# The first steps of a fused attention, mixing and FFT kernel in another order: x ahead of the weights, taps by ScalarE's queue, signs by ScalarE

## The chip, the core and the metric

The kernel runs on one core of one Trainium2 chip. The metric is the device time of one execution in microseconds; for the kernel before there are three runs, and their median counts. A core has engines that each work through their own list of instructions in order: TensorE (PE: matmuls, and PEld: the loads of their weights), VectorE (DVE), ScalarE (ACT), GpSimd (POOL) and SyncE (SP), which here only issues DMA transfers. ScalarE issues some transfers too; in rows of the profile such an issue is marked ACTq, one of SyncE SPq. An instruction that waits for another engine or a transfer holds up everything behind it on its own engine.

## The reference, cut to what matters

```python
B, S, D = 4, 4224, 192
# 1: softmax over 7 taps of 8 heads, a causal convolution of each head's 24 channels
w = softmax(weight)                           # (8, 7)
x = einsum('hk,bskhg->bshg', w, windows(x))   # (4, 4224, 192)
# 2: token mixing of rank 32, then an MLP 192 -> 768 -> 192
h = x^T @ U @ V                               # U (4224, 32), V (32, 4224)
u = x + h^T
x = u + relu(u @ moe_w_ch1) @ moe_w_ch2
# 3: real part of a 2D FFT over sequence and channels, layer norm, a second MLP
u = x + real(fft(fft(x, axis=1), axis=2))
out = u + relu(norm(u) @ moe2_w_ch1) @ moe2_w_ch2
```

The weights of the MLPs, U and V come in as float64, in two 32-bit words each, and the kernel makes float32 of them by integer operations ("decoding").

## The kernel before

Work is cut by batch b (4) and by block j of 384 tokens (11 per batch). For each pair the MLP of stage 2 (s = 0) and, later, of stage 3 (s = 1) runs as one block: layer 1 is six units of matmuls with 384 columns (L665, L655), whose results ScalarE evicts with a relu in half precision (L650) and VectorE as the rest (L651); layer 2 is three units of matmuls with 192 columns (L697 to L701), which VectorE adds to the tokens (L704). Each float32 operand is split into a high and a low half-precision part.

Before the first block can run, much has to be made, and this start is what the change touches:

- The convolution. The taps' softmax runs on single-row tiles (L983 to L989); the row is written to DRAM (L991) and read back as a shifted matrix `tap` by two loads (L995). x comes in three chunks per batch (`load_x`, L159, 14, 14 and 10 columns; three buffers, so chunk 0 of batch 1 takes the buffer of chunk 0 of batch 0). A chunk is convolved in four units (L398, 16 rows of matmuls each), ScalarE evicts each unit in place (L404), and the chunk is stored to DRAM as `x1d` (L368). A gunit (L414) multiplies a chunk by U; VectorE sums the three (L419, L421); `gfin` (L427, L431) replicates the sum.
- A block (`pre1`) loads its tokens from `x1d` (`pre_load`, L504), adds h (matmul L522, add L525), takes the sizes (ScalarE, L543), the scales (L547, L550), the normalised copy and its high half (ScalarE, L555, L578), the low half (GpSimd, L561), and transposes both by DMA (L585) into `ch`, which layer 1 reads.
- Decoding (`decode`, L162): five VectorE instructions per piece of up to 384 columns: the sign taken off (L172), a clamp (L175), a shift (L176) and two merges (L178, L179). A weight piece is followed by its maximum (L223). `weights_units(0)` makes from this the scale (L230 to L243; the maximum over partitions takes a matmul, L121) and the splits: split1h, split1e (ScalarE, L257) and split1a, split1b (VectorE, L264, L286 to L296) for w1, split2 for w2.

The order of all this is written by hand. `play(0)` goes through the words of `START[0]`; a word like c4 takes four steps from the queue c (convolution of batch 0), d is batch 1's convolution, w the weights' steps, a and b the first and second block's steps, e the split of V; X, U, V, P, Y, L are loads, A0 and s0 the stores of the first 4 and the other 10 columns of chunk 0, u0, u1, v0 decodings, B0 and B1 (`busy`) idle matmuls that fill TensorE's waits, as the `WARM` matmuls at the very start do. `START[t]` for t > 0 is played between the units of the blocks. The program order of each engine follows from it; what two engines owe each other is awaited where the later one stands in its list. ScalarE issues A0 in the kernel before; SyncE issues all else here.

Of the kernel before, what the change touches and what calls it, by code (L numbers as in the profile page):

```python
# [6 lines left out]
F32 = mybir.dt.float32  # L7
# [37 lines left out]
WARM = 52  # L45
AGAIN = (18, 44)
# [51 lines left out]
def build(tc, io):  # L98
# [30 lines left out]
    with tc.manual_schedule():  # L129
# [32 lines left out]
        def decode(raw, out):  # L162

            p, n = raw.shape[0], raw.shape[1]
            if n > DN:
                decode(raw[:, :DN], out[:, :DN])
                decode(raw[:, DN:], out[:, DN:])
                return
            lo, hi = raw[:, :, 0], raw[:, :, 1]
            t = wrk.tile([P, DN], I32, name="dec", bufs=1)[:p, :n]  # L170
            g, h = nc.vector.tensor_scalar, nc.vector.scalar_tensor_tensor
            g(out=t, in0=hi, scalar1=0x7FFFFFFF, scalar2=None, op0=ALU.bitwise_and)  # L172

            f = t.bitcast(F32)
            g(out=f, in0=f, scalar1=W_MIN, scalar2=W_MAX, op0=ALU.max, op1=ALU.min)  # L175
# [13 lines left out]
        def weights_units(i):  # L189
# [31 lines left out]
            def dec(a, z, n):  # L221
                decode(st["raw"][:, a:z], st["w"][:, a:z])
                nc.vector.tensor_reduce(out=st["mx"][:, n:n + 1], in_=st["w"][:, a:z],  # L223
                                        axis=AX.X, op=ALU.max, apply_absolute_value=True)
# [83 lines left out]
            if i == 0:  # L308
# [3 lines left out]
                                       lambda: scaled(0, FF + FH, 0), split1h, split1e, split1a, split1b] + \  # L312
# [188 lines left out]
        def pre_load(b, j):  # L501
            t = wrk.tile([P, TB, D], F32, name="u", tag="u", bufs=5)
            src = x1d[b]
            nc.sync.dma_start(  # L504
# [455 lines left out]
        part = w0_st["st"]["part"]  # L960
        part(0)
        load_uv("u", 0, UH)
# [28 lines left out]
        nc.sync.dma_start(rowd[:, nz:KC * H], rowt[:, nz:])  # L991

        load_x(0, 0)
        for i in range(2):
            nc.sync.dma_start(tap[KC * i:KC * i + KC].rearrange("p o h -> p (o h)"), bass.AP(  # L995
# [5 lines left out]
        def dec_u(n):  # L1001
            sl = slice(n * UH, (n + 1) * UH)
            decode(uv["u"][:, sl], uf[:, sl])

        def dec_v(a, z):
# [8 lines left out]
                    s0=lambda: stores[0](0, FIRST), A0=lambda: stores[0](0, 0, FIRST, nc.scalar))  # L1014
        for n in range(4):
            jobs.update({f"X{n}": lambda n=n: load_x(0, n), f"Y{n}": lambda n=n: load_x(1, n),
                         f"P{n}": lambda n=n: part(n), f"L{n}": lambda n=n: ahead_load(n),
                         f"s{n + 1}": lambda n=n: stores[0](n + 1),                          f"u{n}": lambda n=n: dec_u(n)})

        def play(t):  # L1020
# [117 lines left out]
```

## Time and profile before

| what | us |
|---|---|
| median of 3 runs | 1028.82 |
| lowest, highest | 1028.32, 1030.73 |
| profiled execution: span from first to last instruction | 1017.3 |
| TensorE busy | 979.1 |
| VectorE busy | 748.4 |
| ScalarE busy | 604.4 |
| GpSimd busy | 380.9 |

The whole device time of the profiled execution isn't given beside its span; the median is 11.5 us above that span. A row of a timeline gives the start, the duration, the engine, the line, the operation, the written tile and the read ones, the shapes, and in brackets how long the engine had been idle before and what ended it. The chain of waits is the work that ended last, followed back from the end: at each step what released it.

### The profile page before, as it was taken

What the parts mean: (1) busy time and instruction counts of PE and PEld (TensorE: products, weight loads), DVE (VectorE), ACT (ScalarE), POOL (GpSimd) and SP (SyncE); (2) the same over time, 40 slices, a digit from 0 to 9 for tenths busy, and PEclk for the clock granted to TensorE, in tenths of its full rate; (3) what the DMA queues carried; (4) which work ended last, traced back from release to release, by engine and by line L of the source; (5) the groups of instructions that cost most, each with busy time, mean ns of one, the idle gap of its engine ahead of it and who ended that gap; (6) DMA issues with size and microseconds to landing.
All of it is one profiled execution on the core that took longest, in us unless ns stands there. A gap on an engine that the chain in (4) does not pass through costs nothing.

```text
span 1017.3 us, 25682 instructions
## 1 busy us (share of the span) xinstructions
PE 979.1 (96%) x9929; PEld 764.8 (75%) x9929; DVE 748.4 (74%) x2094; ACT 604.4 (59%) x1512; POOL 380.9 (37%) x397
## 2 busy tenths in 40 slices
PE   8789898999899999999999999998999999999998
PEld 5466676777677777877778887776888877877776
DVE  7766577689876656687776777897789787766663
ACT  2556554765676666656576666655656665555552
POOL 0111111253552344265534445564157651562110
PEclk9999999999999999999999999999999999999999
DMA  7596857685536666443425455433344332542332
GB/s 288 155 230 183 252 148 189 178 213 158 151 99 154 203 201 179 114 138 101 102 73 146 134 155 139 108 87 82 87 131 110 107 87 65 137 110 68 82 72 63
DMA packets 190804, 139.28 MB, mean 137 GB/s; under 512 B 128186, under 2 KB 164257, under 8 KB 189913
## 3 DMA queue, kind: packets, MB, share of 16 engines
q1 hardware_dynamic: 183095, 124.59, 45.6%
q0 software_dynamic: 7104, 12.70, 4.8%
q8 instruction: 77, 1.26, 0.5%
q14 instruction: 46, 0.38, 0.1%
q10 hardware_dynamic: 482, 0.35, 0.1%
HBM read 61.69 MB, written 46.11 MB: 106 GB/s over the span
## 4 chain that ended last, share of the span: by engine, by line
PE 62%; DVE 12%; DMA 11%; POOL 5%; issue 5%; ACT 4%; SPq 0%; DVEq 0%; ACTq 0%; POOLq 0%
PE l L665 24%; PE l L697 9%; PE l L701 8%; PE l L699 8%; PE l L655 5%; DMA ch<-sp 4%; DVE hl L651 3%; DMA xm<-x2d,mrow 2%; POOL xm L756 2%; PE cv L398 2%; PE sd L863 2%; PE s L879 2%; DMA x1d<-xw 1%; DVE x L790 1%; POOL xp L804 1%
## 5 line engine op out<-in xcount | busy, mean ns | idle before, releaser
L665 PE MATMUL l<-ch,w1h 128*128 128x384 f16 x1584 | 407.2, 327 | 15.4 <-DMA ch<-sp 10.1
L697 PE MATMUL l<-w2h,hh 128*128 128x192 f16 x1584 | 391.9, 247 | 5.8 <-DVE hl L651 4.5
L699 PE MATMUL l<-w2l,hh 128*128 128x192 f16 x1584 | 391.4, 247 | 1.2 <-DVE w2l L264 1.2
L701 PE MATMUL l<-w2h,hl 128*128 128x192 f16 x1584 | 391.4, 247 | 0.5 <-DVE hl L651 0.4
L651 DVE SCALAR_TENSOR_TENSOR hl<-l,hh 128x384 f16<-128x384 f32 x528 | 267.6, 549 | 127.2 <-ACT hh L650 126.1
L650 ACT ACTIVATE hh<-l 128x384 f16<-128x384 f32 x528 | 235.3, 494 | 155.7 <-PE l L655 155.3
L665 PEld LDWEIGHTS <-w1h 128*128 128x128 f16 x1584 | 155.1, 98 | 106.8 <-DMA ch<-sp 12.3
L697 PEld LDWEIGHTS <-hh 128*128 128x128 f16 x1584 | 155.6, 98 | 23.1 <-issue 12.3
L665 PE MATMUL l<-ch,w1l 128*128 128x384 f16 x528 | 172.7, 327 | 0.0
L699 PEld LDWEIGHTS <-hh 128*128 128x128 f16 x1584 | 155.7, 98 | 17.1 <-issue 6.5
L701 PEld LDWEIGHTS <-hl 128*128 128x128 f16 x1584 | 155.7, 98 | 3.1 <-DVE hl L651 1.4
L561 POOL TENSOR_TENSOR sp<-un,sp 128x576 f16<-128x576 f32 x44 | 57.3, 1302 | 250.4 <-ACT sp L578 228.3
L655 PE MATMUL l<-ch,w1l 128*128 128x384 f16 (+1 forms) x528 | 133.9, 327 | 0.0
L756 POOL DMA_INDIRECT xm<-x2d,mrow x84 | 84.9, 1011 | 21.3 <-issue 17.8
L631 POOL TENSOR_TENSOR sp<-un,sp 128x576 f16<-128x576 f32 x34 | 44.9, 1320 | 120.2 <-ACT sp L578 118.9
L625 ACT ACTIVATE un<-u,mr,rs 128x192 f32<-128x192 f32 x132 | 62.4, 537 | 25.3 <-DVE mr L619 24.7
L555 ACT ACTIVATE un<-u,rc 128x192 f32<-128x192 f32 x132 | 50.2, 445 | 43.0 <-DVE rc L550 43.0
L704 DVE SCALAR_TENSOR_TENSOR u<-l,cmax,u 128x192 f32<-128x192 f32 x132 | 54.5, 413 | 25.5 <-PE l L701 20.9
L665 PEld LDWEIGHTS <-w1l 128*128 128x128 f16 x528 | 51.8, 98 | 28.0 <-issue 4.0
L543 ACT ACTIVATE junk<-u 128x192 f16<-128x192 f32 x132 | 47.7, 361 | 40.6 <-DVE u L534 24.2
L849 POOL DMA_INDIRECT u<-x2d,mrow x64 | 62.4, 975 | 15.3 <-issue 11.7
L704 DVE SCALAR_TENSOR_TENSOR u<-l,ws,u 128x192 f32<-128x192 f32 x132 | 53.9, 410 | 18.2 <-PE l L701 18.0
(136 smaller groups left out, 1189.5 us busy)
## 6 DMA issues: line engine op xcount, KB each, us to landing
x2d<-u SPq DMA_DIRECT2D x68, 288.0 KB
u<-x1d SPq DMA_DIRECT2D x44, 288.0 KB
out_d<-u SPq DMA_DIRECT2D x43, 288.0 KB
x1d<-xw SPq DMA_DIRECT2D x36, 210.0 KB
u<-x2d SPq DMA_DIRECT2D x32, 192.0 KB
x<-x2d SPq DMA_DIRECT2D x60, 99.0 KB
xw<-x_d SPq DMA_DIRECT2D x4, 1344.0 KB
xw<-x_d SPq DMA_DIRECT2D x8, 672.0 KB
```

The costliest lines, as they stand in the source:

```text
L561: low_engine(0, b, j).tensor_tensor(out=sp[:, :, D:2 * D], in0=k["un"], in1=sp[:, :, :D], op=ALU.subtract)
L625: nc.scalar.activation(un[:, t], u[:, t], AF.Identity, scale=k["r"][:, t:t + 1], bias=k["m"][:, t:t + 1])
L650: nc.scalar.activation(hh[:, m], acc[m], AF.Relu)
L651: nc.vector.scalar_tensor_tensor(out=hl[:, m], in0=acc[m], scalar=0.0, in1=hh[:, m], op0=ALU.max, op1=ALU.subtract)
L655: nc.tensor.matmul(acc[m].rearrange("p (r n) -> p r n", r=TB), lhsT=w["l1"][rows, n, m * P:(m + 1) * P], rhs=kd[x][rows], start=False, sto ...
L665: nc.tensor.matmul(o, lhsT=w[v][:, e, ms], rhs=kd[x], start=(n == 0), stop=False)
L697: nc.tensor.matmul(o, lhsT=hh[:, m, rs], rhs=w["h2"][:, m], start=(m == 0), stop=False)
L699: nc.tensor.matmul(o, lhsT=hh[:, m, rs], rhs=w["l2"][:, m], start=False, stop=False)
L701: nc.tensor.matmul(o, lhsT=hl[:, m, rs], rhs=w["h2"][:, m], start=False, stop=(m == NM - 1))
L704: nc.vector.scalar_tensor_tensor(out=u[:, r], in0=o, scalar=sc, in1=u[:, r], op0=ALU.mult, op1=ALU.add)
L756: nc.gpsimd.indirect_dma_start(out=xs[c][1][:, g], out_offset=None, in_=x2d[b][:], in_offset=bass.IndirectOffsetOnAxis(ap=mrow[:99, k:k + ...
L849: nc.gpsimd.indirect_dma_start(out=u2[:, s0 + 2 * e], out_offset=None, in_=src[:], in_offset=bass.IndirectOffsetOnAxis(ap=mrow[:, k2 + e - ...
```

## The change

- x chunk 0 and the first half of U are loaded ahead of the first weights.
- The row of taps and the two loads of taps are issued by ScalarE's queue instead of SyncE's; so is the load of block 0's tokens (L0).
- In the decoding of the first three weight pieces and of U the sign is taken off by ScalarE (Abs) instead of VectorE; the decoding's scratch tile has two buffers instead of one.
- `START` has another order: the loads of x chunks 1 and 2 and of V ahead of the third weight piece's, w2's load (P2) right behind the stores, chunk 1's stores and chunk 0 of batch 1 (Y0) early, the third piece and its scale behind the second gunit, split1a ahead of split1e, four units of batch 1's convolution (d2 twice) ahead of the first block, w2's scale and split one step earlier.
- `WARM` is 42 for 52 matmuls, the second filler 30 for 44.

```diff
-WARM = 52
-AGAIN = (18, 44)
+WARM = 42
+AGAIN = (18, 30)
...
-        def decode(raw, out):
+        def decode(raw, out, first=False):
...
-            t = wrk.tile([P, DN], I32, name="dec", bufs=1)[:p, :n]
+            t = wrk.tile([P, DN], I32, name="dec", bufs=2)[:p, :n]
             g, h = nc.vector.tensor_scalar, nc.vector.scalar_tensor_tensor
-            g(out=t, in0=hi, scalar1=0x7FFFFFFF, scalar2=None, op0=ALU.bitwise_and)
-
             f = t.bitcast(F32)
+            if first:
+                nc.scalar.activation(f, hi.bitcast(F32), AF.Abs)
+            else:
+                g(out=t, in0=hi, scalar1=0x7FFFFFFF, scalar2=None, op0=ALU.bitwise_and)
...
-                decode(st["raw"][:, a:z], st["w"][:, a:z])
+                decode(st["raw"][:, a:z], st["w"][:, a:z], i == 0 and z <= FF + FH)
...
-                                       lambda: scaled(0, FF + FH, 0), split1h, split1e, split1a, split1b] + \
+                                       lambda: scaled(0, FF + FH, 0), split1h, split1a, split1e, split1b] + \
...
-        def pre_load(b, j):
+        def pre_load(b, j, eng=nc.sync):
...
         part = w0_st["st"]["part"]
+        load_x(0, 0)
+        load_uv("u", 0, UH)
         part(0)
-        load_uv("u", 0, UH)
...
-        nc.sync.dma_start(rowd[:, nz:KC * H], rowt[:, nz:])
-
-        load_x(0, 0)
+        nc.scalar.dma_start(rowd[:, nz:KC * H], rowt[:, nz:])
         for i in range(2):
-            nc.sync.dma_start(tap[KC * i:KC * i + KC].rearrange("p o h -> p (o h)"), bass.AP(
+            nc.scalar.dma_start(tap[KC * i:KC * i + KC].rearrange("p o h -> p (o h)"), bass.AP(
...
-            decode(uv["u"][:, sl], uf[:, sl])
+            decode(uv["u"][:, sl], uf[:, sl], True)
...
+                    L0=lambda: pre_load(0, 0, nc.scalar))
...
         START = [
-            "S U1 P1 X1 X2 V w2 u0 c4 B0 A0 L0 s0 L1 P2 u1 w c5 w3 v0 c4 w c3 w2 a4 w a4 b2 B1 w b4 w L2 b2 w",
-            "w s1", "", "w2 L3 V12", "w s2", "Y0", "z", "", "z", "d", "d Y1", "d", "d z", "d", "d z", "d Y2", "d e", "d", "d e", "d e",
-            "d e", "d e", "d e", "d", "d e", "d e", "d e", "d"]
+            "X1 U1 S X2 V P1 u0 w2 c4 B0 A0 s0 P2 L0 u1 c5 L1 s1 Y0 v0 c4 w c2 w3 c w a3 w a5 w2 B1 b4 w b4 w d2 w L2 d2",
+            "w2", "", "w2 L3 V12", "s2", "Y1", "z", "", "z", "d", "d", "d z Y2", "d", "d z", "d", "d e", "d", "d e", "d", "d e",
+            "d e", "d e", "e", "d", "e", "d e", "e"]
```

## Rows read from the trace of the kernel before

**Rows 1.** The page's first part: busy time, share of the span, instructions.

```profile
PE 979.1 (96%) x9929; PEld 764.8 (75%) x9929; DVE 748.4 (74%) x2094; ACT 604.4 (59%) x1512; POOL 380.9 (37%) x397
```

**Rows 2.** Stretches: length, busy time of each engine, TensorE's granted clock, DMA share, GB/s.

```profile
42.20:60.00 17.80, 13.51 (x87) 8.28 (x87) 15.03 (x40) 11.46 (x31) 2.56 (x2) 0.95 0.67 187
60.00:70.00 10.00, 8.70 (x81) 7.18 (x79) 6.68 (x20) 3.28 (x9) 0.02 (x1) 0.91 1.10 266
```

**Rows 3.** Timeline of TensorE: a filler, and starts after a wait.

```profile
16.09 3.10 PE L975 MATMUL l<-hl 128*128 128x384 f16 x18
...
42.20 0.32 PE L665 MATMUL l<-ch,w1h 128*128 128x384 f16 x1 [2.67 <-DMA ch<-sp]
...
58.30 0.29 PE L699 MATMUL l<-w2l,hh 128*128 128x192 f16 x1 [1.21 <-DVE w2l L264]
...
65.78 0.34 PE L665 MATMUL l<-ch,w1h 128*128 128x384 f16 x1 [1.30 <-DVE xmax L712]
```

**Rows 4.** The chain of waits in order of time: start, length, what.

```profile
4.48 2.02 DMA rowd<-hh
...
7.19 6.36 DMA tap<-rowd
13.59 0.92 PE cv L398 x15
```

**Rows 5.** Timeline of ScalarE.

```profile
14.49 2.85 ACT L404 ACTIVATE xw<-cv 128x336 f32<-128x336 f32 x8 [10.97 <-PE cv L398]
17.37 1.77 ACTq L368 DMA_DIRECT2D x1d<-xw  x2
...
31.20 1.29 ACT L257 ACTIVATE w1h<-u,sc 64x384 f16<-64x384 f32 x2
...
35.48 1.15 ACT L555 ACTIVATE un<-u,rc 128x192 f32<-128x192 f32 x3 [1.54 <-DVE rc L550]
36.65 0.68 ACT L578 ACTIVATE sp<-un 128x576 f16<-128x576 f32 x1
```

**Rows 6.** Timeline of SyncE's queue: the load of block 0.

```profile
24.49 0.33 SPq L504 DMA_DIRECT2D u<-x1d  x1
```

**Rows 7.** Waits of SyncE's queue up to 60 us: total, times, longest.

```profile
SPq L504 <- DMA x1d<-xw: 19.7, 3, 10.5
...
SPq L159 <- DMA xw<-x_d: 1.9, 1, 1.9
```

**Rows 8.** DMA from 17.4 to 20.7 us: the only queue with data packets.

```profile
q1 hardware_dynamic: 207, 1.31, 95.4%
```

**Rows 9.** DMA from 20.7 to 24.4 us: ScalarE's queue (q10) and SyncE's (q1).

```profile
q10 hardware_dynamic: 476, 0.34, 27.7%
q1 hardware_dynamic: 122, 0.34, 22.8%
```

**Rows 10.** Timeline of VectorE: the decoding and its waits.

```profile
5.15 0.36 DVE L172 TENSOR_SCALAR dec<-u 128x384 int32<-128x384 int32 x1 [0.70 <-DMA u<-wa_d]
...
10.90 0.35 DVE L172 TENSOR_SCALAR dec<-u 128x384 int32<-128x384 int32 x1
...
15.52 0.36 DVE L172 TENSOR_SCALAR dec<-u 128x384 int32<-128x384 int32 x1 [0.51 <-DMA u<-u_d]
...
24.35 0.36 DVE L419 COPY gacc<-gp 128x192 f32<-128x192 f32 x1 [1.75 <-PE gp L414]
...
25.37 0.29 DVE L122 TENSOR_REDUCE ma<-am 128x1 f32<-128x128 f32 x1 [0.60 <-PE am L121]
...
28.95 0.36 DVE L421 TENSOR_TENSOR gacc<-gp,gacc 128x192 f32<-128x192 f32 x1 [0.67 <-PE gp L414]
29.93 0.36 DVE L421 TENSOR_TENSOR gacc<-gp,gacc 128x192 f32<-128x192 f32 x1 [0.62 <-PE gp L414]
...
39.67 0.36 DVE L172 TENSOR_SCALAR dec<-u 128x384 int32<-128x384 int32 x1 [3.44 <-DMA u<-wc_d]
...
48.48 0.55 DVE L223 TENSOR_REDUCE mx<-u 128x1 f32<-128x384 f32 x1
...
56.83 1.42 DVE L264 SCALAR_TENSOR_TENSOR w2l<-u,sc,w2h 128x1152 f16<-128x1152 f32 x1 [2.28 <-ACT w2h L257]
```

**Rows 11.** An Abs on ScalarE (its timeline); a convolution unit of batch 1 (chain).

```profile
32.51 0.36 ACT L543 ACTIVATE junk<-u 128x192 f16<-128x192 f32 x1
...
78.96 0.79 PE cv L398 x16
```

More of the change, by code (lines that the diff above doesn't have):

```diff
@@ L159, in load_x @@
             nc.sync.dma_start(xw_t[b, c][:, ks], io["x"][b, c][:, ks])
-        def decode(raw, out):
+        def decode(raw, out, first=False):
             p, n = raw.shape[0], raw.shape[1]
             if n > DN:
-                decode(raw[:, :DN], out[:, :DN])
-                decode(raw[:, DN:], out[:, DN:])
+                decode(raw[:, :DN], out[:, :DN], first)
+                decode(raw[:, DN:], out[:, DN:], first)
                 return
             lo, hi = raw[:, :, 0], raw[:, :, 1]
-            t = wrk.tile([P, DN], I32, name="dec", bufs=1)[:p, :n]
+            t = wrk.tile([P, DN], I32, name="dec", bufs=2)[:p, :n]
             g, h = nc.vector.tensor_scalar, nc.vector.scalar_tensor_tensor
-            g(out=t, in0=hi, scalar1=0x7FFFFFFF, scalar2=None, op0=ALU.bitwise_and)
             f = t.bitcast(F32)
+            if first:
+                nc.scalar.activation(f, hi.bitcast(F32), AF.Abs)
+            else:
+                g(out=t, in0=hi, scalar1=0x7FFFFFFF, scalar2=None, op0=ALU.bitwise_and)
             g(out=f, in0=f, scalar1=W_MIN, scalar2=W_MAX, op0=ALU.max, op1=ALU.min)
@@ L499, in build @@
         xmax = {}
-        def pre_load(b, j):
+        def pre_load(b, j, eng=nc.sync):
             t = wrk.tile([P, TB, D], F32, name="u", tag="u", bufs=5)
             src = x1d[b]
-            nc.sync.dma_start(
+            eng.dma_start(
                 t, src[j * TB * P:(j + 1) * TB * P].rearrange("(p r) d -> p r d", r=TB))
@@ L1013, in build @@
                     U1=lambda: load_uv("u", UH, 2 * UH),
-                    s0=lambda: stores[0](0, FIRST), A0=lambda: stores[0](0, 0, FIRST, nc.scalar))
+                    s0=lambda: stores[0](0, FIRST), A0=lambda: stores[0](0, 0, FIRST, nc.scalar),
+                    L0=lambda: pre_load(0, 0, nc.scalar))
         for n in range(4):
             jobs.update({f"X{n}": lambda n=n: load_x(0, n), f"Y{n}": lambda n=n: load_x(1, n),
-                         f"P{n}": lambda n=n: part(n), f"L{n}": lambda n=n: ahead_load(n),
+                         f"P{n}": lambda n=n: part(n), f"L{n + 1}": lambda n=n: ahead_load(n + 1),
                          f"s{n + 1}": lambda n=n: stores[0](n + 1),                          f"u{n}": lambda n=n: dec_u(n)})
```

## Prediction

> **What bounds the kernel now.** I read the page first: TensorE is busy for 96% of the span [rows 1], so after its start the kernel can only gain what TensorE no longer has to do. The stretches come next: between 42.20 and 60.00 us TensorE is busy for 13.51 of 17.80 us and its granted clock is 0.95, so some of that stretch ran at 1.2 GHz and the rest at 2.4 GHz [rows 2]. Then TensorE's timeline: the first layer-1 matmul starts at 42.20 us, the second layer gets going only at 58.30 us, when VectorE's low half of w2 is there, and one more wait of 1.30 us ends at 65.78 us [rows 3]. Everything that is moved lies ahead of 58.30 us, so the question is when that point comes, and how much work for TensorE is left after it.
>
> Two chains lead there. The chain of waits shows the first: the row of taps takes 2.02 us to DRAM, and the two tap loads that follow it hold the first convolution until 13.59 us, 6.36 us after the second was issued [rows 4]. ScalarE empties the four units (14.49 to 17.34 us) and issues the first two stores at 17.37 us [rows 5]; SyncE, which must see them landed before it may load block 0, gets past them at 24.49 us [rows 6], a wait of 10.5 us for that load alone [rows 7]. The second chain is VectorE. From 15.52 us to 49.03 us (the last maximum, 48.48 plus 0.55) it does one long list: half of U, the third weight piece, V, the splits, the adds of two blocks, three pieces of w2. In it are waits of 1.75, 0.60, 0.67, 0.62 and 3.44 us [rows 10], 7.08 us in all, so 26.43 us are work.
>
> **Part by part.**
>
> *x first, taps on ScalarE's queue.* x chunk 0 is no longer behind two loads, but the convolution needs the taps as well, and those set its start. Their row can't leave before the softmax is done, which nothing here makes earlier: 4.48 us as before [rows 4]. The warm-up has 10 matmuls fewer; 18 of the same kind took 3.10 us at the full granted clock [rows 3], so that is 1.7 us, and TensorE is free at about 11.1 us instead of 12.8. That is the lower end of the convolution's start. The upper end is not given by 13.59 us alone: the taps now share the DMA engines with the loads that SyncE has already queued, instead of standing behind x chunk 0 only. How such a transfer fares is seen once: of the two stores that ScalarE's queue issued at 17.37 us, no packet at all moved until 20.7 us, while SyncE's queue moved 207 [rows 8]; from then both moved [rows 9]. So about 3.3 us pass before the first packet. Twice 3.3 us (the row of taps, then the taps) on 4.48 us, with their landing, gives 12 to 14 us. I take 12.5 us, 1.1 us earlier than now; bounds 11.1 and, with more queued ahead, 17.5 us.
>
> *Stores and the load of block 0 on ScalarE's queue.* ScalarE issues the stores 3.78 us after the convolution's start (13.59 to 17.37) [rows 4, 5], that is at 16.3 us. The load of block 0 now stands behind them on **ScalarE** and waits there for their landing, and so does all that ScalarE has queued next: the signs of the second half of U and the eight evictions of x chunk 1. That is the new wait. Before, it was SyncE that stood still, with the remaining stores of chunk 0 and w2 behind it. Its price: the same two stores took 7.12 us from issue to the next step (17.37 to 24.49) [rows 5, 6]; the nearest lower bound is the tiny row of taps, 2.02 us [rows 4]. I take 7.1 us, the row of the very same transfers, since SyncE's queue is full at that time in the new order as well. ScalarE goes on at 23.4 us; bounds 18.3 and 24.5 us, or 28 with the late taps.
>
> *Signs by ScalarE.* Seven VectorE instructions of 0.28 to 0.36 us go (three weight pieces, two halves of U with two pieces each). What they cost on ScalarE is bounded by the 0.36 us of an Abs of half the width [rows 11] and twice that; I take 0.5 us. Up to 23.4 us VectorE has the first half of U and two weight pieces. Before, the two weight pieces took 5.75 us (5.15 to 10.90) and half of U 4.11 us (10.90 to 15.01) [rows 10]; without the signs 5.0 and 3.4 us. Begun when ScalarE has issued the taps, at about 8.5 us, they end at 17 us. VectorE then **stands still for about 6.9 us**, because its next job, the other half of U, waits for its sign.
>
> *VectorE's list from there.* It is the same list as from 15.52 to 49.03 us: 26.43 us of work less three signs (1.1 us), 25.35 us. Its waits are others. w2 now leaves SyncE's queue right behind the stores and lands long before it is wanted, so the 3.44 us are gone. The waits for the gunits' matmuls (1.75, 0.67, 0.62) are covered by V and the third weight piece. New are 0.5 us for the first sign of U, 0.5 us for that of the third piece, 0.6 us for the maximum's matmul (as before), about 0.8 us for the chain from the last add to block 0's add, which the split no longer covers, and the wait for the split of the two ends, which ScalarE now does after block 0's normalised copy: 1.15 + 0.68 + 1.29 us [rows 5], of which I count 2.8. That is 5.2 us. The list ends at 23.4 + 25.35 + 5.2 = 54.0 us, **5.0 us later** than 49.03.
>
> *From the list's end to TensorE's steady work.* Before, 9.27 us (49.03 to 58.30). In the new order w2's scale and split come one step earlier, which can save up to the 1.42 us of that split [rows 10]; against it the eight evictions of the moved convolution units, 2.85 us on ScalarE [rows 5], stand ahead of the first relus. Bounds -1.4 and +2.9 us; I take +1.2.
>
> *Work moved ahead.* Four units of batch 1's convolution now run before the first block. Each took 0.79 us in TensorE's chain [rows 11], so 4 x 0.79 = **3.2 us less** is left after that point; TensorE waits there anyway, so they cost nothing if chunk 0 of batch 1 has landed by then; its load stands behind chunk 1's stores, and if it comes late the first layer waits for it, and the 3.2 us are the bound of that too. The shorter second filler (30 for 44) is idle work in the same wait: nothing.
>
> *The wait at 65.78 us.* It was VectorE's backlog behind the late split of w2; with that split a step earlier I let it go: -1.3 us; bounds -1.3 and 0.
>
> **Sum**: +5.0 +1.2 -3.2 -1.3 = +1.7 us on a span of 1017.3 us. What lies around the span is 1028.82 - 1017.3 = 11.5 us, if the profiled execution is like the median of the three runs, and nothing there is touched. So 1028.82 + 1.7 = 1030.5 us. About 0.3%, 3.1 us, is what a measurement of this kernel can tell from no change; this is inside it.
>
> **The rivals.**
>
> *Faster: the stores land soon.* The Trainium skill, "DMA: Bandwidth & Descriptors", section "Queues, rings and completion order", says that a DMA engine goes round-robin between the queue rows that have work, a packet at a time. [Rows 8] speak against that for the first 3.3 us, [rows 9] for it afterwards. As a mechanism of this kernel: if ScalarE's transfers get their share at once, the taps are there when the warm-up ends (11.1 us), the stores leave at 14.9 us and land in about 3.7 us, the length of the stretch in which they moved [rows 9], at 18.6 us. ScalarE goes on 4.8 us earlier than in my sum: 1025.7 us. If TensorE then has no stretch at 1.2 GHz between 42 and 70 us, another 0.05 x 17.8 + 0.09 x 10 = 1.8 us could come back [rows 2]; with half of that, **1024.8 us**. It decides for itself where ScalarE goes on before about 19 us.
>
> *Slower: the taps come late.* SyncE waited 1.9 us with a load of x for an earlier load of x that has its own tile [rows 7]: a transfer waits for one some places ahead of it, whatever they hold. In the new order five or six large loads are issued ahead of the taps. If a tap load waits for x chunk 1 in this way, or the engines take up SyncE's queued loads first, the convolution starts at 17.5 us instead of 12.5 and all that follows moves by 5 us: **1035.5 us**. For it: the taps sat behind everything that was ahead of them before as well. Against: rows 9, and that 3.3 us is what was seen. It decides where the convolution starts after about 14 us.
>
> *The change doesn't do what it says*: x is first, but the taps gate the convolution. That is already part of my sum; it gives 1.1 us.
>
> **How the numbers follow.** My own case, 1030.5 us with a range of 1027.5 to 1033, gets 0.42; faster 0.28 at 1024.8; slower 0.30 at 1035.5. The part of my case above 1031.9 and that of the slower case below it are about equal. So faster by over 0.3% 0.28, within 0.3% 0.41, slower by over 0.3% 0.31. The range reaches into both rivals and leaves 1 in 10 out on each side: 1023.5 to 1037.
>
> **What would show it.** On ScalarE's timeline: the load of block 0 issued some 7 us after the two stores, and nothing between. On VectorE: a wait of 5 to 8 us that a sign of the second half of U ends, and no wait for w2. The first convolution at 11 to 14 us. The last maximum of w2 near 54 us. TensorE's second layer from about 64 to 66 us, and four convolution units of batch 1 ahead of the first layer-1 matmul. My sum is wrong if ScalarE goes on before 19 or after 26 us, or if VectorE's list, from that sign on, isn't about 30 us long.

## The result, and the profile after

| | median, us | lowest to highest | profiled execution: its time, span |
|---|---|---|---|
| before | 1029.78 | 1028.32 to 1035.2 | not given, 1017.3 |
| after | 1041.2 | 1040.38 to 1042.84 | 1040.38, 1038.6 |

The ratio is 1.0105, interval 1.0067 to 1.0144: the change costs 0.0105 x 1029.78 = 10.8 us. I had forecast +1.7 us and a range that ended at 1037.

The two spans differ by 21 us, not by 11. What lies around the span of after is 1040.38 - 1038.6 = 1.8 us (1.7 to 2.7 in all other runs). If it is as much before, the 11.5 us of my sum were no time around the span: the profiled execution of before was 1028.82 - 1017.3 - 1.8 = 9.7 us quicker than the median beside it. Chips differ: the kernel before had a median of 1028 us on one and of 1015 to 1017 us on three others. Below, ratios compare runs of the same chip, and a second pair of traces, before (span 1026.2) and after (1039.3) on one chip, stands for the first where a difference of few us matters.

Timeline of TensorE after, three starts that a wait precedes (start, length, what, in brackets the idle time and what ended it):

```profile
15.96 5.64 PE L400 MATMUL cv<-xw,tap 64*64 64x168 f32 x64 [5.65 <-DMA tap<-rowd]
...
57.51 0.48 PE L667 MATMUL l<-ch,w1h 128*128 128x384 f16 x1 [4.51 <-ACT xw L406]
...
62.44 0.77 PE L121 MATMUL am<-sel,mx 128*128 128x128 f32 x2 [1.57 <-DVE mx L232]
```

Before, the first convolution began at 13.59 us and the first layer-1 matmul at 42.20 [rows 3, 4]. The convolution took 2.57 us there and takes 5.64 here. The stretches (length, busy time of each engine, granted clock, DMA share, GB/s) say why: the clock is 0.50, that is 1.2 GHz, after 5.65 us in which TensorE had nothing to do; and it is 0.50 again as the blocks begin (before, 0.95 and 0.91 between 42 and 70 us [rows 2]).

```profile
16.20:20.30 4.10, 4.03 (x54) 3.08 (x57) 2.39 (x6) 1.59 (x4) 0.00 (x0) 0.50 0.98 392
...
56.70:66.90 10.20, 7.82 (x27) 3.63 (x27) 7.38 (x20) 4.51 (x12) 1.28 (x1) 0.50 0.67 186
```

ScalarE's timeline after shows the new wait. The stores leave at 22.45 us (17.37 before [rows 5]), the load of block 0 behind them at 29.88, and only then the sign of U's second half:

```profile
8.72 1.14 ACTq L996 DMA_DIRECT2D tap<-rowd  x2
...
22.45 0.90 ACTq L370 DMA_DIRECT2D x1d<-xw  x2
29.88 0.37 ACTq L506 DMA_DIRECT2D u<-x1d  x1
30.35 0.84 ACT L174 ACTIVATE dec<-u 128x384 f32<-128x384 f32 x2 [7.92 <-DMA x1d<-xw]
```

From the issue of the stores to that of the load behind them are 29.88 - 22.45 = 7.43 us, hardly more than before (7.12), but they are spent in another way. The DMA from 22.4 to 23.4 us (its busy share in 40 slices, in tenths), then what moved from 22.4 to 25.7 us (queue, packets, MB, share of the 16 engines; q10 is ScalarE's queue, q1 SyncE's):

```profile
DMA  0000000000000000000000000000000000004457
...
q1 hardware_dynamic: 417, 0.32, 37.8%
q10 hardware_dynamic: 224, 0.17, 20.9%
```

The DMA engines were idle when the stores were issued. The first packet of ScalarE's queue moved at 23.64 us, 1.2 us after the issue and not 3.4 as before; from then to 29.4 us the stores shared the engines with SyncE's stores of the rest of chunk 0 and w2's load, which left SyncE at 22.45 and 23.35 us.

VectorE's timeline after: it stands still for 12.20 us, and its last maximum of w2 ends at 60.75 + 0.55 = 61.30 us, 12.3 us later than the 49.03 of [rows 10].

```profile
10.49 0.36 DVE L177 TENSOR_SCALAR dec<-dec 128x384 f32<-128x384 f32 x1 [6.03 <-ACT dec L174]
...
30.93 0.36 DVE L177 TENSOR_SCALAR dec<-dec 128x384 f32<-128x384 f32 x1 [12.20 <-ACT dec L174]
...
48.34 0.98 DVE L296 COPY w1h<-w1h 64x384 f16<-64x384 f16 x1 [2.46 <-ACT w1h L259]
...
60.75 0.55 DVE L225 TENSOR_REDUCE mx<-u 128x1 f32<-128x384 f32 x1
...
71.00 1.42 DVE L266 SCALAR_TENSOR_TENSOR w2l<-u,sc,w2h 128x1152 f16<-128x1152 f32 x1 [0.96 <-ACT w2h L259]
```

The taps: issued at 8.72 and 9.26 us, they moved no packet for over three microseconds. First the DMA from 9.0 to 12.2 us, then from 12.2 to 16.0:

```profile
q1 hardware_dynamic: 145, 1.35, 100.7%
...
q1 hardware_dynamic: 279, 0.85, 70.7%
q10 hardware_dynamic: 158, 0.26, 28.8%
```

In the second pair of traces the last maximum ends at 61.81 us after (first row) against 47.46 before, 14.35 us later:

```profile
61.26 0.55 DVE L225 TENSOR_REDUCE mx<-u 128x1 f32<-128x384 f32 x1
...
46.91 0.55 DVE L223 TENSOR_REDUCE mx<-u 128x1 f32<-128x384 f32 x1
```

From the eleventh block's transposes on, the transposes start 10.1 to 15.9 us later, those of the last block 13.3, and the spans differ by 13.1. So the whole loss is there before TensorE's steady work begins, and of the 14.35 us only 1.25 are given back by the end.

### The profile page after: what moved, and what is told of

Same layout as the page of the kernel before. It is cut to its first block, busy times and chain, and to the rows that moved or that the text cites. A ratio compares the mean times of both kernels' runs of the same rounds, so it can differ in the third digit from the quotient of the medians.

```text
span 1038.6 us, 25637 instructions
## 1 busy us (share of the span) xinstructions
PE 983.1 (95%) x9905; PEld 765.1 (74%) x9905; DVE 743.9 (72%) x2087; ACT 604.3 (58%) x1519; POOL 380.3 (37%) x397
## 4 chain that ended last, share of the span: by engine, by line
PE 53%; DVE 8%; issue 5%; DMA 5%; POOL 5%; ACT 1%; POOLq 0%; DVEq 0%; SPq 0%; ACTq 0%
PE l L667 21%; PE l L699 8%; PE l L703 7%; PE l L701 7%; PE l L657 4%; DMA ch<-sp 3%; DVE hl L653 3%; POOL xm L758 2%; DMA xm<-x2d,mrow 2%; PE sd L865 1%; PE s L881 1%; PE s L825 1%; POOL xp L806 1%; DVE x L792 1%; DVE u L706 1%
## 5 line engine op out<-in xcount | busy, mean ns | idle before, releaser
L699 PEld LDWEIGHTS <-hh 128*128 128x128 f16 x1584 | 155.2, 98 | 23.9 <-issue 12.4
L706 DVE SCALAR_TENSOR_TENSOR u<-l,ws,u 128x192 f32<-128x192 f32 x132 | 53.9, 410 | 24.0 <-PE l L703 12.2
L851 POOL DMA_INDIRECT u<-x2d,mrow x64 | 62.0, 969 | 15.3 <-issue 12.2
```

Of the source, the lines that this page charges most:

```text
L699: nc.tensor.matmul(o, lhsT=hh[:, m, rs], rhs=w["h2"][:, m], start=(m == 0), stop=False)
L706: nc.vector.scalar_tensor_tensor(out=u[:, r], in0=o, scalar=sc, in1=u[:, r], op0=ALU.mult, op1=ALU.add)
L851: nc.gpsimd.indirect_dma_start(out=u2[:, s0 + 2 * e], out_offset=None, in_=src[:], in_offset=bass.IndirectOffsetOnAxis(ap=mrow[:, k2 + e - ...
```

## The experiments

Ratios are to the kernel before on the same chip; 0.001 is about 1 us. The last column is the end of w2's last maximum, that of VectorE's list, in the one trace of each run, in us; it is 49.03 and 47.46 in the two traces of before and 61.30 in the first trace of after.

| run | what it is | ratio | interval | list ends |
|---|---|---|---|---|
| e7 | after, again | 1.0131 | 1.0103 to 1.0158 | 61.81 |
| e1 | after, load of block 0 on SyncE | 1.0055 | 1.0036 to 1.0074 | 55.41 |
| e2 | after, taps on SyncE | 1.0102 | 1.0069 to 1.0135 | 57.96 |
| e3 | after, 76 warm-up matmuls | 1.0099 | 1.0071 to 1.0127 | 60.24 |
| e4 | after, signs on VectorE | 1.0086 | 1.0056 to 1.0116 | 59.29 |
| h2 | after, w2's scale and split in their old place | 1.0111 | 1.0092 to 1.0129 | 61.83 |
| e5 | after, load and taps on SyncE, 52 warm-up matmuls | 1.0047 | 1.0029 to 1.0065 | 51.71 |
| g1 | e5, signs on VectorE | 1.0060 | 1.0044 to 1.0075 | 52.11 |
| h1 | e5, w2's steps in their old place | 1.0047 | 1.0031 to 1.0062 | 51.84 |
| h3 | h1, four conv units in their old place | 1.0033 | 1.0016 to 1.0050 | 52.90 |
| k1 | h3, x chunk 0 in its old place | 1.0039 | 1.0021 to 1.0057 | 51.83 |
| e6 | e1, four conv units in their old place | 1.0067 | 1.0044 to 1.0090 | 55.17 |
| f1 | before, load of block 0 on ScalarE | 1.0035 | 1.0023 to 1.0047 | 51.56 |
| f2 | before, signs on ScalarE | 1.0001 | 0.9985 to 1.0016 | 48.94 |
| g2 | before, w2's load, scale and split earlier | 1.0038 | 1.0010 to 1.0067 | 47.98 |
| k2 | before, x chunk 0 and U first | 1.0026 | 1.0008 to 1.0045 | 51.45 |
| h4 | before, rest of V loaded later | 1.0006 | 0.9992 to 1.0021 | 48.92 |

How much later than 48.25 us (the mean of the two traces of before) the list ends, and how much time the run loses, lie within 2.3 us of each other in every run but g2: 7.2 and 5.6 us in e1, 13.6 and 13.5 in e7, 3.3 and 3.6 in f1, 0.7 and 0.1 in f2. In g2 the list ends no later and 3.9 us are lost; what is lost there is TensorE's, as shown below. With one trace of each run this is a pattern over many kernels, not a test of any single part.

### After and before once more

> The kernel after itself, unchanged, beside the kernel before on the same chip. If the ratio 1.0105 belongs to the change and not to the chip: 1.009 to 1.012, and its trace shows the start as seen (first convolution near 16 us, ScalarE goes on near 30 us, last maximum near 61 us); the further 9 us by which the two first traces drift apart between blocks 32 and 88 are not there. Rival (the drift belongs to the change): a trace that loses time between 400 and 1000 us against the kernel before's trace of this chip.

> The kernel before itself, unchanged, for a trace from the same chip as the runs beside it: span within 0.3% of its own timed runs, first convolution near 13.6 us, last maximum near 49 us, first layer-1 matmul near 42 us.

After came out a little above what was expected, 1.0131, and before as expected: the loss belongs to the change, and the further 9 us by which the first two traces drift apart don't. In this trace of before w2 came sooner: VectorE waited 1.23 us for it, not 3.44 [rows 10].

### The load of block 0 on ScalarE's queue

```diff
-                    L0=lambda: pre_load(0, 0, nc.scalar))
+                    L0=lambda: pre_load(0, 0))
```

> The kernel after with one thing undone: the load of block 0's tokens is issued by SyncE again. Theory 1 (the load, waiting for the stores on ScalarE's queue, holds ScalarE 7.4 us, from 22.4 to 29.9, and with it the signs of U's second half and VectorE's list): ScalarE does those signs right after the evictions, near 22.7 us, VectorE's idle time ahead of that clamp falls from 12.20 to about 5 us, its last maximum comes near 51 us instead of 57.97, and 5 to 7 us of time come back: 1034 to 1036 us. Rival (the late taps and TensorE at 1.2 GHz set the time, and ScalarE's stop lies beside the same wait on SyncE): the signs come earlier but the first layer-1 matmul stays within 2 us of 57.5, and the time stays at 1040 to 1042 us.

(The 57.97 us in it is the end of the last maximum but one; the last one ends at 61.30.) The theory held: the ratio falls from 1.0105 or 1.0131 to 1.0055, 5 to 8 us come back, the largest price of any single part. VectorE, in that run:

```profile
23.83 0.36 DVE L177 TENSOR_SCALAR dec<-dec 128x384 f32<-128x384 f32 x1 [5.14 <-ACT dec L174]
...
54.86 0.55 DVE L225 TENSOR_REDUCE mx<-u 128x1 f32<-128x384 f32 x1
```

The idle time falls from 12.20 to 5.14 us, the last maximum comes 5.9 us earlier, and so does the first layer-1 matmul (51.61 us). The same edit alone in the kernel before:

```diff
-        def pre_load(b, j):
+        def pre_load(b, j, eng=nc.sync):
...
+                    L0=lambda: pre_load(0, 0, nc.scalar))
```

> The kernel before with one part of the change alone: the load of block 0's tokens is issued by ScalarE's queue. VectorE takes its own signs off here. Theory (the load stops ScalarE until the stores have landed; the signs are what carries that stop to VectorE): ScalarE stands from 17.8 to about 24.5 us, the evictions of x chunk 1 come 2 to 4 us later, VectorE waits that much longer for the gunits' matmuls, and the time is 1.5 to 4 us over the kernel before, 1.0015 to 1.004 of it. Rival (the stop is all of it, with or without the signs): 6 us or more, 1.006 or above.

The theory held: 1.0035. ScalarE stands there too, from the stores at 16.84 to 25.16 us. But VectorE decodes on by itself; it meets the stop only at the first gunit, whose chunk the evictions behind the load make late (6.83 us of waiting there, 1.75 in [rows 10]). SyncE gains by it: w2's load leaves at 27.48 us, not at 31.95, and VectorE's wait of 3.44 us for w2 is gone, so the 3.5 us are what is left after that gain:

```profile
25.16 0.36 ACTq L504 DMA_DIRECT2D u<-x1d  x1
25.62 2.85 ACT L404 ACTIVATE xw<-cv 128x336 f32<-128x336 f32 x8 [8.81 <-DMA x1d<-xw]
...
28.95 0.36 DVE L419 COPY gacc<-gp 128x192 f32<-128x192 f32 x1 [6.83 <-PE gp L414]
```

### The signs

```diff
-            decode(uv["u"][:, sl], uf[:, sl], True)
+            decode(uv["u"][:, sl], uf[:, sl])
...
-                decode(st["raw"][:, a:z], st["w"][:, a:z], i == 0 and z <= FF + FH)
+                decode(st["raw"][:, a:z], st["w"][:, a:z])
```

> The kernel after with one thing undone: the signs of the decoding are taken off by VectorE again (seven instructions of 0.28 to 0.36 us). Theory (the signs tie VectorE's list to ScalarE, which stands behind the load of block 0): VectorE decodes U's second half right behind the weight pieces, near 19 us, and its idle time of 12.20 us is gone; what it then waits for is x chunk 1's convolution, whose evictions stand behind the same load, so part comes back: the last maximum near 53 us, time 1034 to 1038 us. Rival (the evictions of x chunk 1 alone hold the list; the signs do nothing): VectorE only stops one step later, and the time is 1040 to 1043 us.

The wait for a sign is gone, but what replaces it is nearly as long: 10.86 us for the first gunit's matmul, behind the same stop of ScalarE:

```profile
32.75 0.36 DVE L421 COPY gacc<-gp 128x192 f32<-128x192 f32 x1 [10.86 <-PE gp L416]
...
58.74 0.55 DVE L225 TENSOR_REDUCE mx<-u 128x1 f32<-128x384 f32 x1
```

The last maximum ends at 59.29 us, 2.0 us earlier than after and not the 8 that I expected; the time, 1.0086, can't be told from that of after. Nor do the signs cost anything alone in the kernel before, where the same lines are put in with the second buffer of `dec`:

> The kernel before with one part of the change alone: the signs of the first three weight pieces and of U are taken off by ScalarE, with two buffers for the decoding's scratch. Theory (a sign on ScalarE stands behind the evictions and the stores of x chunk 0 there): the signs of U's second half come near 18 us instead of VectorE's own at 15.5, VectorE idles 3 us more and has 2 us less of work, and the time is within 0.3% of the kernel before, 0.999 to 1.003. Rival (the signs save what they weigh on VectorE, 2.1 us): 0.998 or below.

VectorE idles 5.54 us for the first sign of U's second half and makes up for it later; its list ends at 48.94 us:

```profile
19.65 0.36 DVE L177 TENSOR_SCALAR dec<-dec 128x384 f32<-128x384 f32 x1 [5.54 <-ACT dec L174]
```

In these two places the signs carry someone else's lateness and cost nothing of their own that the time shows.

### Taps and clock

```diff
-        nc.scalar.dma_start(rowd[:, nz:KC * H], rowt[:, nz:])
+        nc.sync.dma_start(rowd[:, nz:KC * H], rowt[:, nz:])
...
-            nc.scalar.dma_start(tap[KC * i:KC * i + KC].rearrange("p o h -> p (o h)"), bass.AP(
+            nc.sync.dma_start(tap[KC * i:KC * i + KC].rearrange("p o h -> p (o h)"), bass.AP(
```

> The kernel after with one thing undone: the row of taps and the two tap loads are issued by SyncE again, so x chunk 1, U's second half, sel and x chunk 2 leave SyncE's queue behind them. Theory (the taps come late because they share the engines with loads that are queued ahead of them): the first convolution starts near 13.5 us as in the kernel before instead of 15.96, TensorE's wait ahead of it falls from 5.65 to about 3.3 us; ScalarE's stores leave 2.4 us earlier, and if the convolution then runs at 2.4 GHz 3 us more. Time 1036 to 1039 us. Rival (ScalarE's stop behind the stores alone makes the time, and the stores land when the queue is free, whenever they were issued): the convolution starts earlier but ScalarE still goes on near 30 us, and the time stays within 1.5 us of 1041.

```diff
-WARM = 42
+WARM = 76
```

> The kernel after with 76 instead of 42 warm-up matmuls, so that TensorE is busy until about 16 us, when the taps land. Theory (the shorter warm-up left TensorE idle 5.65 us, and its granted clock fell to 0.50 for the first convolution, 5.64 us instead of 2.57): the convolution runs at 2.4 GHz, 2.5 to 3 us shorter, the stores leave that much earlier, ScalarE goes on near 27 us; time 1037.5 to 1039 us. Rival (the clock falls for another reason, or the stores' landing doesn't follow their issue): the convolution still takes over 4 us, or ScalarE still goes on near 30 us, and the time stays at 1040 to 1042 us.

TensorE in e2, then in e3, then e3's stretch:

```profile
12.98 5.70 PE L400 MATMUL cv<-xw,tap 64*64 64x168 f32 x64 [2.42 <-DMA tap<-rowd]
```

```profile
16.63 2.57 PE L400 MATMUL cv<-xw,tap 64*64 64x168 f32 x62 [0.58 <-DMA tap<-rowd]
...
16.70:19.20 2.50, 2.50 (x63) 2.32 (x64) 1.96 (x4) 1.67 (x5) 0.00 (x0) 1.00 0.98 404
```

Both mechanisms show as expected: with the taps on SyncE's queue the convolution starts 3 us earlier, with TensorE kept busy it runs at 2.4 GHz in 2.57 us. ScalarE goes on at 26.99 and 28.18 us instead of 30.35; the last maximum ends 3.3 and 1.1 us earlier. The times, 1.0102 and 1.0099, lie within the interval of after, so that these 1 to 3 us come back in the time isn't shown. No run undoes both and leaves the load of block 0 on ScalarE, where they hold up most; what the two cost together there is read from the trace of after alone.

### The three together

The edits of e1 and e2, and:

```diff
-WARM = 42
+WARM = 52
```

> The kernel after with three things undone: the load of block 0 and the row of taps with its two loads are issued by SyncE again, and the warm-up has 52 matmuls. The rest of the change stays (x first, signs by ScalarE, the other order with four units of batch 1 ahead). Theory (all the loss comes from ScalarE's stop behind the stores and from the late, slow first convolution): the convolution starts near 13 us at 2.4 GHz, the stores leave near 17 us, VectorE idles under 2 us ahead of U's second half, its last maximum comes near 49 us, and the time is within 0.3% of the kernel before, 0.997 to 1.002 of it. Rival (the other order itself costs: the early units of batch 1 wait for their chunk and their evictions hold the first layer-1 matmul): the time stays 0.4% or more above the kernel before, with the first layer-1 matmul 4 us or more behind the second block's first transposes' landing.

1.0047: 6 to 9 us of the loss are the load, the taps and the warm-up, nearly all of them the load (e1: 1.0055, on another chip; the list ends 3.7 us earlier here than there, of which the two ratios don't show more than 1 us). The theory is missed; the time is the rival's. VectorE still idles 4.16 us, the conv units wait 5.05 us for their chunk, and one more wait appears that was not in any sum of mine: 3.15 us of TensorE for w2's maximum.

```profile
43.18 4.29 PE L400 MATMUL cv<-xw,tap 64*64 64x168 f32 x64 [5.05 <-DMA xw<-x_d]
...
52.85 0.46 PE L121 MATMUL am<-sel,mx 128*128 128x128 f32 x2 [3.15 <-DVE mx L232]
```

With the signs undone as well:

> The kernel with the load of block 0 and the taps on SyncE's queue and 52 warm-up matmuls (1.0047 of the kernel before), less one thing more: the signs go back to VectorE. What is left of the change is x first and the other order with four units of batch 1 ahead. Theory (the signs still cost there: VectorE idled 4.16 us for one): VectorE starts U's second half near 17 to 18 us instead of 21.25, its last maximum comes 1.5 to 3 us earlier than 51.7 us, and the time is 1.001 to 1.004 of the kernel before. Rival (the order is what is left): 1.004 to 1.006, and the conv units of batch 1 still wait 4 us or more for their chunk.

1.0060: the rest lies in the order, as the rival has it, or in x first, which this run keeps too, though the conv units wait only 2.35 us for their chunk here.

### The other order, step by step

w2's load behind the stores, its scale and split a step earlier, alone in the kernel before:

```diff
-            "S U1 P1 X1 X2 V w2 u0 c4 B0 A0 L0 s0 L1 P2 u1 w c5 w3 v0 c4 w c3 w2 a4 w a4 b2 B1 w b4 w L2 b2 w",
-            "w s1", "", "w2 L3 V12", "w s2", "Y0", "z", "", "z", "d", "d Y1", ...
+            "S U1 P1 X1 X2 V w2 u0 c4 B0 A0 L0 s0 P2 L1 u1 w c5 w3 v0 c4 w c3 w2 a4 w a4 b2 B1 w b4 w L2 b2 w",
+            "w2 s1", "", "w2 L3 V12", "s2", "Y0", "z", "", "z", "d", "d Y1", ...
```

> The kernel before with two small parts of the change alone: w2 is loaded behind the stores, ahead of block 1's load, and w2's scale and split come one step earlier. If my reading of VectorE's list holds (it sets TensorE's steady work, and it waits 1.2 to 3.4 us for w2), its wait for w2 is under 0.5 us, its last maximum comes 1 to 3 us earlier, and the time is 0.997 to 0.999 of the kernel before. Rival (block 1's load, now behind w2 on the queue, comes late and holds the adds instead): 1.000 to 1.002, with a wait of VectorE for that load.

VectorE's list does end 1 us earlier (47.98), w2's wait is gone, and 1.62 us of it come back as a wait for block 1's load, as the rival had it. But the time is 1.0038, worse than either. TensorE's waits between 40 and 70 us (what waited, for what, total, times, longest):

```profile
PE am L121 <- DVE mx L230: 5.1, 1, 5.1
PE l L665 <- DMA ch<-sp: 2.7, 1, 2.7
```

The maximum over partitions is a matmul (L121). A step earlier it stands ahead of four layer-1 units in TensorE's order, and TensorE waits 5.06 us there for VectorE's last maximum; three of the units behind it run at 44.45 to 47.1 us in the kernel before. After this wait the granted clock is 0.50. The stretch from 50 to 54 us in g2, then in the kernel before:

```profile
50.00:54.00 4.00, 4.00 (x17) 1.87 (x18) 1.97 (x8) 0.49 (x1) 0.00 (x0) 0.50 0.93 246
...
50.00:54.00 4.00, 4.00 (x30) 2.38 (x28) 3.90 (x16) 3.06 (x11) 0.00 (x0) 1.00 0.91 229
```

TensorE ran 17 matmuls instead of 30 in the same four us: it loses time by the wait and by the clock behind it. In the kernel after, the same wait is the 1.57 us at 62.44. Undoing this step in e5 (h1) and in after (h2):

```diff
-            "w2", "", "w2 L3 V12", "s2", ...
+            "w", "", "w2 L3 V12", "w s2", ...
```

> The kernel with the load of block 0 and the taps on SyncE's queue and 52 warm-up matmuls (1.0047 of the kernel before), less one thing more: w2's scale and split stand where the kernel before has them. Theory (the matmul of w2's maximum, a step earlier, stands ahead of layer-1 units and TensorE waits 3.15 us there for VectorE's last maximum): that wait is gone, layer-1 units of block 0 and 1 run on, and the time falls by 2.5 to 4 us, to 1.001 to 1.0025 of the kernel before. Rival (the four conv units that wait for their chunk are what is left): the time stays at 1.004 to 1.006.

> The kernel after with one thing undone: w2's scale and split stand where the kernel before has them. Theory: TensorE's wait for the maximum's matmul (1.57 us, and 0.95 us of VectorE's for it) is gone, but the first layer-1 matmul still comes at 57 to 58 us; the time falls by 1.5 to 3 us, to about 1.009 to 1.010 of the kernel before where the kernel after is 1.0105 to 1.013. Rival (the early split saves what I gave it, 1.3 us and more): the time rises by 1 us or more.

My theory fell: 1.0047 and 1.0111, nothing comes back that these runs can tell. In h1 that wait of TensorE is gone, but VectorE now waits 2.10 us for block 2's tokens:

```profile
54.93 0.89 DVE L527 TENSOR_TENSOR u<-h,u 128x192 f32<-128x192 f32 x3 [2.10 <-DMA u<-x1d]
```

Their load (L2) stands behind both blocks' transposes in the new order and leaves SyncE at 50.44 us; before, it left between the two, at 40.27. The four conv units back in their old place, in e1 (e6) and in h1 (h3), with four more d among the later words:

```diff
-            "... B1 b4 w b4 w d2 w L2 d2",
+            "... B1 b4 w b4 w w L2",
```

> The kernel with the load of block 0 on SyncE's queue (the run above that moved it alone), less one thing more: the four units of batch 1's convolution come in their old place, after the blocks have begun. Theory (in that kernel the units wait 2.97 us for their chunk, run at half the clock for 3.81 us, and hold the first layer-1 matmul 2.32 us by their evictions): the first layer-1 matmul comes 4 to 5 us earlier, near 47 us, the 3.2 us of work come back later, and the time falls by 1 to 2 us against that run, to 1.0035 to 1.0045 of the kernel before. Rival (the units are work done in a wait, as my prediction had it): the time rises by up to 3.2 us, to 1.0065 to 1.009.

> The run above that has both w2's old place and the start of the kernel before for taps, load and warm-up, less one thing more: the four units of batch 1's convolution stand in their old place. What is left of the change is x first, the signs by ScalarE and the order of loads. Theory (the units wait 5 us for their chunk and run at 1.2 GHz, which costs about as much as moving them saves): within 1.5 us of that run, and within 0.3% of the kernel before, 0.998 to 1.002; the first layer-1 matmul comes near 42 to 43 us. Rival (the units are work done in a wait): 3 us above that run.

In e6 the first layer-1 matmul comes at 46.51 instead of 51.61 us, and yet the time doesn't fall: 1.0067 against 1.0055. In h3 it falls a little, 1.0033 against 1.0047. All intervals overlap: moving the units is worth nothing that these runs can tell, in either direction. Last, x first, alone in the kernel before (k2), and the reverse in h3 (k1):

```diff
+        load_x(0, 0)
+        load_uv("u", 0, UH)
         part(0)
-        load_uv("u", 0, UH)
...
-        load_x(0, 0)
```

> The kernel before with one part of the change alone: x chunk 0 and the first half of U are loaded ahead of the first weights; the taps stay on SyncE's queue behind them. Theory (the row of taps stands behind 2.8 MB instead of 1.4): it lands near 10 us instead of 6.6, the first convolution starts 0.3 us earlier to 1 us later, all loads behind the taps leave 3.5 us later, VectorE starts 3 to 4 us later, and the time is 2 to 5 us over the kernel before, 1.002 to 1.005 of it. Rival (all of that lies in waits that are there anyway, as my sum had it): 0.999 to 1.001.

> The kernel of 1.0033 (load, taps' queue, warm-up, w2's place and the four conv units undone), less one thing more: the first weights are loaded first again and x chunk 0 leaves behind the row of taps. What is left of the change is the signs by ScalarE, the order of the later loads and a shorter second filler. Theory (x chunk 0 ahead of the row of taps holds that row, and with it SyncE's later loads, 3.5 us): the row lands near 6.7 us instead of 10.2, VectorE starts at 5 to 6 us instead of 8.6, U's second half lands 3 us earlier, and the time is 0.998 to 1.001 of the kernel before. Rival (the order of the later loads is what is left): 1.002 to 1.004.

Alone in the kernel before it costs 2.6 us, as the theory had it. The row of taps lands only before 10.21 us (SyncE issues the taps there; at 6.60 before), and VectorE's first weights come 4.8 us later than the 5.15 of [rows 10]:

```profile
9.96 0.36 DVE L172 TENSOR_SCALAR dec<-u 128x384 int32<-128x384 int32 x1 [5.50 <-DMA u<-wa_d]
```

In k1 the row lands by 6.62 us as expected, but the time stays, 1.0039: the rival holds there. So about 4 us of the loss (2 to 6 by the interval) are in what k1 still has of the change. It is not one step that undoing brings back; block 2's load behind the transposes and the splits' order (a wait of 2.45 or 2.46 us for ScalarE in every kernel with it) are candidates that I could only argue, not test alone. The signs are a third: in k1 VectorE's list begins at 19.50 us, 4.0 us later than the 15.52 of [rows 10], behind a sign that ScalarE does only after its evictions and the stores.

```profile
19.50 0.36 DVE L177 TENSOR_SCALAR dec<-dec 128x384 f32<-128x384 f32 x1 [4.16 <-ACT dec L174]
```

f2 shows no price of the signs in the old order and g1 none beside x first; k1 with its signs on VectorE wasn't run.

### An attempt at a better version

```diff
-            "w s1", "", "w2 L3 V12", "w s2", "Y0", "z", "", "z", ...
+            "w s1", "", "w2 L3", "w s2", "V12 Y0", "z", "", "z", ...
```

> The kernel before with one new edit, not part of the change: the load of the rest of V leaves SyncE's queue behind block 2's transposes instead of ahead of them. TensorE waits 2.99 us (1.30 us in the first trace) near 64 us in the kernel before, and the transposes' issue takes 5.3 us while that load and chunk 2's stores fill the engines. If the load is what holds them, the transposes land 2 to 3 us earlier and the time is 0.997 to 0.9985 of the kernel before. Rival (the stores hold them, or the rest of V then comes late for its decoding): 0.999 to 1.002.

No gain, 1.0006: VectorE then waits 7.12 us for the rest of V. No kernel here was measurably faster than the one before.

## Why the prediction was wrong, point by point

The step that failed is the time at which ScalarE goes on behind the stores: 23.4 us in the sum, 30.35 in the trace, past the 26 us that I had named as the sign of a wrong sum and past the 28 of the late taps. Two terms ahead of it were wrong, the convolution's start (point 3) and TensorE's clock (point 4). They make 6.2 of the 7.0 us by which ScalarE, and with it VectorE's list, came late. The 3.3 us that I gave back behind the list were too much as well (point 6).

1. *What bounds*: right. The time of the steady work follows the end of VectorE's list, and a list that ends 12 to 14 us later makes a kernel 11 to 13 us slower; the other runs fit, but for g2.
2. *The list itself*: right. From ScalarE's going on to the last maximum I had 54.0 - 23.4 = 30.6 us; it took 61.30 - 30.35 = 30.95. From its end to w2's low half 9.27 + 1.2 = 10.5; it took 72.42 - 61.30 = 11.1.
3. *The convolution's start*, 12.5 us taken, 15.96 measured, was mis-sized, within its bounds. The wait for the first packet was right: 3.3 us taken, and 3.7 from 8.72 to 12.4. What I left nearly out is the time from a first packet to the landing: I gave it 12.5 - 4.48 - 6.6 = 1.4 us for row and taps together, and the taps alone need 3.5, since SyncE's queue moves 279 packets beside their 158. [Rows 9] had shown such sharing.
4. *The clock* was not in the sum, and that step failed outright. I took 1.7 us off for ten matmuls fewer and never asked what TensorE does between their end and the taps. It idles 5.65 us, and the convolution takes 3.07 us longer. Nor had I the second stretch at 0.50, from 56.7 to 66.9 us, with 7.82 us of TensorE's work in it; at 1.00 that work would take half (an estimate), but no run shows what it costs the time.
5. *The stores to their landing*: 7.1 us taken, 7.43 measured, but by luck. My reason was that SyncE's queue is full at that time in the new order as well. It was not: the engines were idle, the first packet came after 1.2 us, and the rest is sharing with SyncE's stores and w2's load, which the new order issues at the same time. ScalarE's going on, 23.4 taken, 30.35 measured, is late by 7.0: 3.5 of point 3, 2.7 of point 4 (the evictions hide the rest), 0.8 of smaller things. This is the term that carries the miss: 7.0 of the 7.3 us by which the list's end was wrong.
6. *Work moved ahead and the wait at 65.78*: I gave back 3.2 + 1.3 - 1.2 = 3.3 us after the list's end; the second pair of traces gives back 14.35 - 13.1 = 1.25. These 2 us and the 7.3 of the list's end make up about the 9.1 us between +1.7 and +10.8. As an edit of its own the moved work shows no gain (e6, h3).
7. *w2's split a step earlier*: I saw only what it saves VectorE and not the matmul in TensorE's order that comes with it. With w2's load moved too, in the kernel before, it costs 3.8 us (g2). The place of block 2's load I had not priced at all.
8. *x first* I had as neutral but for the taps. Alone it costs 2.6 us (k2).
9. *Rivals*: the slower one had the right sign and the right point (the convolution starts after 14 us), but I held its price to 5 us. Its mechanism, a transfer that waits for one some places ahead, appeared on another queue. SyncE's waits up to 60 us in after:

```profile
SPq L324 <- DMA tap<-rowd: 7.3, 1, 7.3
```

The load of V, on SyncE's queue, waited 7.3 us for a tap load, which was now on ScalarE's; V is decoded only from 34.40 us on, so VectorE did not wait for it. The faster rival rested on ScalarE's transfers getting their share at once. The Trainium skill, "DMA: Bandwidth & Descriptors", section "Issuing engines are not separate DMA queues", says that transfers started by different engines run on the same 16 DMA engines and interleave, and that another issuing engine saves only issue time. The trace agrees with the first half only from 12.4 us on: from 9.0 to 12.2 us it has 145 packets of SyncE's queue and none of ScalarE's. It agrees with the second in that no time was won: with the taps on ScalarE's queue the convolution starts at 15.96 us, on SyncE's (e2) at 12.98; that it starts later is in neither half.

The four parts tried alone in the kernel before, 3.5 + 0.1 + 3.8 + 2.6 thousandths, add up to 10.0, near the 10.5 to 13.1 of the whole. But the taps' queue and the warm-up aren't among them, and undone one by one in the kernel after, only the load gives much back; so the near agreement doesn't show that the parts add up. Each part's lateness can lie beside another's there.

## What to carry to other kernels

A load that waits for a store should not be issued by an engine that computes (5 to 8 us here in the new order, 3.5 in the old): everything behind it on that engine waits too, and each job that is tied to that engine carries the stop further. When a load moves, price everything that ends up behind it on both queues, and count a small transfer's landing as the wait for its first packet plus its share of the engines; both depend on what else is issued at that moment, so a length read from the old order need not hold in the new one. When TensorE is held by filler work, let its end meet the next real work: here that work ran at half the clock after 2.42 and 5.65 us of idling.

## What the runs showed of the hardware

- A small transfer that ScalarE issued while SyncE's loads were queued moved its first packet 3.4 us (stores, before), 3.5 us (row of taps in after, 4.49 to 8.03; two stores of zeros stood ahead of it on its own queue) and 3.7 us (taps) after its issue. Issued with the engines idle, the stores in after moved theirs after 1.2 us, and then took 5.7 us beside SyncE's transfers for what took 3.2 us before.
- On SyncE's own queue the row of taps took 2.1 us from its issue to that of the taps behind weights and half of U, and 5.7 us with x chunk 0 there too (k2, 4.48 to 10.21).
- A transfer on one queue can wait for one on another: 7.3 us of SyncE for a tap load of ScalarE's.
- The granted clock was 0.50 for the first convolution in after (5.65 us idle ahead of it) and e2 (2.42), and 1.00 in e3 (0.58). What it costs is not always what the time shows: 3.07 us less in e3 left the ratio at 1.0099.
- Executions of one kernel on one chip lie some us apart (1013.02 to 1019.63 us for before beside h1). The two traces of before (perhaps from two chips; that of the first isn't known) agree within 2 us up to block 34 and are 9 us apart at the end: such a drift says nothing of a change at the start.
